# A due time for every operation of a list-planned residual quantizer

## The chip, the core and the metric

The kernel runs on one core of one Trainium2 chip. The metric is the device time of one execution in microseconds, the median of the runs. A core has TensorE (PE) for matrix products, VectorE (DVE) and ScalarE (ACT) for elementwise work, GpSimd (POOL) and SyncE (SP), which here mostly issue transfers, and 16 DMA engines. Each engine works through its own queue in the order in which the program was written; an operation at the head of a queue that waits holds up all that stands behind it.

## The reference

```python
B, T, D, K = 2, 16000, 512, 3
Nq, C = 4, 8
...
z = sum over i of xp[:, i:i+T, :] * dw_enc[i]      # 3 taps along T, per channel
z = silu(z)
res = z; q = 0
for s in range(Nq):
    cb = codebooks[s]                               # 8 words of 512
    d2 = |res|^2 - 2 res.cb + |cb|^2
    sel = cb[d2.argmin(-1)]
    q = q + sel
    res = res - sel
y = sum over i of qp[:, i:i+T, :] * dw_dec[i]      # 3 taps along T, per channel
```

All tensors are bfloat16; `xp` and `qp` are padded by one row at each end of T. A three-tap filter per channel is followed by a SiLU, then by four stages of quantization. Each finds the nearest of 8 code words for every row and subtracts it from the residual. The sum of the chosen words goes through a second three-tap filter.

## The kernel before

The 32000 rows are 128 partitions of 250 rows. A *group* is one row of every partition, so there are 250 groups, worked on in 18 chunks of 4, 12, thirteen times 16, 12, 8 and 6 groups (`SIZES`). A chunk is held transposed, channels on partitions, in four blocks of 128 channels (`KT`); a full block is 128 x 2048 elements.

For each chunk, in order:

- `load`: DMA transposes on SP's queue (L491) bring rows into an `XT` buffer, of which there are two. The first two chunks come by `load_rows`: PE transposes, and copies to `XT` by ACT (L456) for even blocks and by DVE (L454) for odd ones.
- `front`, for each block: three products with the taps (L557 on DVE; L555 on ACT for the middle tap of blocks 0 to TAPS1-1 of the first `FEW` = 6 chunks), two additions (L565 on DVE, or L563, an accumulating transfer that POOL issues: one for each block, two for block 0, none in the first two chunks), then `exp` on ACT (L569), `one` (plus 1, DVE, L576), `inverse` on ACT (a reciprocal, recorded at the helper's line L201), and `silu` on DVE (L584), which writes the residual `RES`. Exponentials and reciprocals need different tables of ACT, which are loaded between them.
- `stage`, four times: products of the residual with itself and the code words on PE (`score`, L654 and L659), in two or three parts for a chunk; maxima and copies on DVE and ACT (L694, L672, L698); the small chain on DVE `with_norm` (L736), `distance` (L742), `least` (L746), `marks` (L751); `turn` and `pairs` on PE (L769, L802) with copies on ACT (L778, L807); `chosen` on PE (L835), which writes the chosen words to PSUM as `SEL`; and `subtract` on DVE (L841). In the fourth stage `settle` takes the place of `pairs` and what follows.
- `finish`: the decoder's products (`Y`, L859), copies to `YSB` by ACT (L865, 126 of them), and stores on SP's queue (L869).

**The planner.** Nothing is issued while these functions run. Each calls `plan.add(engine, hold, delay, needs, due, emit, take, give, use, move)`: the engine and how long it is held, how long until the result can be used, the entries that must be done first, a due time, the function that issues the instructions, and the buffers that are taken and given back. `move` describes a transfer on a shared bus. `Plan.run` then goes through time on these prices. Whenever an engine is free it takes, among the entries whose needs are met and whose buffers are there, the one with the earliest due time, and issues it. The order in which the entries are taken is the order of the program, for each engine; the prices themselves cause nothing on the chip. The engine name `BANK` stands for bookkeeping entries that issue no instruction.

Due times come from a few constants in units of `PERIOD` = 56 planned us: a chunk starts at `org`, 56 us for 16 groups after the one before; products and additions of block i fall due at `org + (i * SPREAD - LEAD) * PERIOD`, `exp` and `one` `EXPS` periods after that, `inverse` and `silu` at `org + AFTER * PERIOD`, stage s at `org + s * STAGE * PERIOD`, and so on. A path-length term, `END - STRETCH * tail`, can only make them earlier.

Two rules of the `front` matter below. An `inverse` needs its own block's `one` and the last `exp` that was added, block 3's; an `exp` needs the last `inverse` of the chunk before:

```python
e = plan.add("ACT", act(1.8) + load, act(1.8) + load + 0.12, [z] + turned[-1:], due + EXPS * PERIOD, exp, take=("E",))
...
e = plan.add("ACT", act(1.8) + load, act(1.8) + load + 0.12, [o, ended[-1]], due, inverse)
```

Here `load` is `SWITCH` = 1.3 for block 0 and 0 for the others, so the plan counts one table load for the exponentials and one for the reciprocals of a chunk.

**Idle products.** When PE would stand still in the plan and has been little used in the last 3.4 planned us, the planner puts in a product whose result nobody reads (`warm`, L432; 229 of them).

Of the kernel before, what the change touches and what calls it, by code (L numbers as in the profile page):

```python
# [37 lines left out]
SWITCH = 1.3  # L38
PERIOD = 56.0
LEAD = 0.269  # L40
SPREAD = 0.081
EXPS = 0.293
AFTER = 0.664
STAGE = 0.861
NEXT = 0.126
LAST = 0.74
LATE = 0.468
HURRY = 0.905
TABLES = -1.436
COLS = 0  # L50
MOVES = 0
END = 1097.406
STRETCH = 2.086
FEW = 6
ONES1 = 0
TAPS1 = 2
ROWS = 2
SUMS = 0
NORMS = 14
NFROM = 2  # L60
NTO = 14
OVER = -0.515
FETCH = 1.963
FAR = -3.3e38


class Plan:
# [7 lines left out]
        self.bus, self.turned = 9.0, 0.0  # L75

    def add(self, engine, hold, delay, needs, due, emit, take=(), give=(), use=1.0, move=None):
        self.tasks.append((engine, hold, delay, [n for n in needs if n is not None], due, emit, take, give, use, move))
        return len(self.tasks) - 1

    def run(self):
        tasks = self.tasks
        left = [len(t[3]) for t in tasks]
        after = [[] for _ in tasks]
        for n, t in enumerate(tasks):
            for d in t[3]:
                after[d].append(n)
        engines = list(dict.fromkeys(t[0] for t in tasks))
        ready = {e: [] for e in engines}
        until = {e: 0.0 for e in engines}  # L90
        tail = [0.0] * len(tasks)
        for n in reversed(range(len(tasks))):
            t = tasks[n]
            tail[n] = max(t[1], t[2] + (t[9][0] if t[9] else 0.0)) + max((tail[a] for a in after[n]), default=0.0)
        dues = [min(t[4], END - STRETCH * tail[n]) for n, t in enumerate(tasks)]
        spans = []
        for n, t in enumerate(tasks):
            if not left[n]:
                heapq.heappush(ready[t[0]], (dues[n], n))
        now, events, order = 0.0, [], []  # L100
        while len(order) < len(tasks):
            going = True
            while going:
                going = False
                for e in engines:
                    if until[e] > now + 1e-9:
                        continue
                    passed, pick = [], None
                    while ready[e]:
                        due, n = heapq.heappop(ready[e])  # L110
                        if all(self.slots[k] > 0 for k in tasks[n][6]):
                            pick = n
                            break
                        passed.append((due, n))
# [24 lines left out]
                    if e == "PE":  # L139
                        spans.append((now, until[e], tasks[pick][8]))  # L140
                    heapq.heappush(events, (now + hold, -1))
                    heapq.heappush(events, (now + max(hold, delay), pick))
                    going = True
            if len(order) == len(tasks):
                break
            now = events[0][0]
            while events and events[0][0] <= now + 1e-9:
                _, n = heapq.heappop(events)
                if n < 0:
                    continue  # L150
                for k in tasks[n][7]:
                    self.slots[k] += 1
                for a in after[n]:
                    left[a] -= 1
                    if not left[a]:
                        heapq.heappush(ready[tasks[a][0]], (dues[a], a))
# [3 lines left out]
def kernel(  # L160
# [310 lines left out]
    def load(st, org):  # L471
# [5 lines left out]
        if st["n"] in plain:  # L477
            st["off"] = g0
            space = plan.add("BANK", 0.0, 0.0, [chunks[0]["space"]], early, lambda: st.update(XT=chunks[0]["XT"]))
            for n in range(g0 + 2, g0 + G + 2):  # L480
                done.append(plan.add("SP", 1.31, 0.9, [space], early + 0.01 * n,
                                     lambda n=n: nc.sync.dma_start_transpose(out=chunks[0]["XT"][:, :, n, :], in_=group_rows(n - 1)),
                                     move=(0.78, True)))
            st["loaded"] = done + chunks[st["n"] - 1]["loaded"]
            return

# [27 lines left out]
        for n in range(2, G + 2):  # L514
            due += 0.01
            inside = 0 <= g0 + n - 1 < S
            t = plan.add("SP", 1.31, 0.9, [space], due, (lambda n=n: one(n)) if inside else (lambda n=n: edge(n)), move=(0.78, True))
            done.append(t)
            if not inside:
                done.append(plan.add("POOL", 1.0, 1.4, [t], due, lambda n=n: shift(n)))  # L520
# [3 lines left out]
    def front(st, org):  # L524
# [21 lines left out]
        def block(i):  # L546
# [41 lines left out]

            def add_up(k, needs):
                if k <= adds:  # L590
                    return plan.add("POOL", 0.9, 1.24, needs, due, lambda: total(k), give=("T",), move=(0.2 + 2.6 * f, False))
                return plan.add("DVE", dve(1.13), dve(1.13) + 0.1, needs, due, lambda: total(k), give=("T",))

            hold, delay = dve(0.67), dve(0.67) + 0.1
# [3 lines left out]
                t = plan.add("ACT", act(2.0), act(2.0) + 0.12, st["loaded"], due, lambda: product(1), take=("T",))  # L598
            else:
                t = plan.add("DVE", hold, delay, st["loaded"], due, lambda: product(1), take=("T",))  # L600
            z = add_up(1, [z, t])
            t = plan.add("DVE", hold, delay, st["loaded"], due, lambda: product(2), take=("T",), give=("XT",) if i == KT - 1 and n >= plain[-1] else ())
            st["taps"].append(t)
            z = add_up(2, [z, t])
            load = 0.0 if ended else SWITCH
# [16 lines left out]

            return rest

        ended, now = [], []
        st["taps"], st["silu"], st["new"] = [], [], {}
        for rest in [block(i) for i in range(KT)]:
            rest()
        begun.extend(now)

    turned, begun, kept = [], [], {}

    def stage(st, s, due):
        G, MB = st["GP"], st["MB"]
# [11 lines left out]

        def score(q, m):
            RES = st["RES"]
            if q == 0:
                u["TR"], u["PR"] = SCORES[turns[0] % len(SCORES)]  # L650
                turns[0] += 1
            PS = pending.pop() if pending else psG.tile([P, 512], F32, name="PS")
# [2 lines left out]
            for e in range(m):  # L655
                for i in range(KT):
                    for h in range(2):
                        half = RES[:, i, 2 * (e % 2 * R + (q + e) // 2) + h, :]
                        nc.tensor.matmul(V[h * HT:(h + 1) * HT, e, :], lhsT=half[:, LC:LC + HT], rhs=half[:, lo:hi],  # L659
                                         start=False, stop=(i == KT - 1), skip_group_check=True)  # L660
            if s == Nq - 1 and q + m == G:
                free["RES"].append(RES)
            if not scored[2:]:
                scored.append(None)

# [36 lines left out]
        for m in ([4], [4, 4], [6, 6], [6, 6, 4])[MB - 1]:  # L702
            needs = [st["new"][i] for i in range(KT)]
            needs += scored[0:2] + ([codes[st["n"]]] if st["n"] < 3 else [])
            t = plan.add("PE", 0.05 + 0.215 * m, 0.25 + 0.215 * m, needs, due, lambda q=q, m=m: score(q, m), take=("psG",),
                         give=("RES",) if s == Nq - 1 and q + m == G else (), use=0.7)
            seen.append(t)
            if apart:
                g = plan.add("ACT", 0.06 + 0.0535 * m, 0.18 + 0.0535 * m, [t], due, lambda q=q, m=m: positive(q, m), take=("G",))
# [9 lines left out]
            plan.add("BANK", 0.0, 0.0, maxima[-2:], due, lambda: None, give=("psG",))  # L719
            q += m  # L720

        if apart:
            first, rest = grams[:-1], grams[-1:]
            t = plan.add("PE", 0.04 * sum(m for _, m, _, _ in first), 0.2 + 0.04 * sum(m for _, m, _, _ in first),
# [88 lines left out]
            t = plan.add("DVE", 0.2, 0.33, maxima, due, with_norm, give=("psA",) if apart else ())  # L813
        t = plan.add("DVE", 0.15, 0.26, [t], due, distance)
        t = plan.add("DVE", 0.2, 0.33, [t], due, least)
        t = plan.add("DVE", 0.2, 0.36, [t] + preset[0:3], due, marks, take=("OH",) if s == 0 else ())
        last = s == Nq - 1
        t = plan.add("PE", 0.05 + 0.06 * MB if last else 0.15, 0.25 + 0.06 * MB if last else 0.33, [t], due, turn, take=("psA",),
                     give=("OH",) if last else ())
# [31 lines left out]
    def outputs(groups, needs, due):  # L851
# [20 lines left out]
        for k in range(0, len(groups), 2):  # L872
# [1 line left out]
            d = [plan.add("PE", 0.22 * count, 0.22 * count + 0.2, needs, due, lambda k=k: decode(k), take=("psA",))]  # L874
            decoded.extend(d[-1:])
            c = plan.add("ACT", 0.93, 1.05, [c, d[-1]], due, lambda k=k: pair(k), take=("Y",) if k == 0 else (), give=("psA",))
        plan.add("SP", 0.35, 1.1, [c], due, store, give=("Y",), move=(0.1 + 0.365 * len(groups), False))

    def edge(name, src, shift):
        t = const.tile([P, P], BF16, name=name)  # L880
# [84 lines left out]
```

## Time and profile before

| what | value |
|---|---|
| three runs | 719.88, 714.88, 717.16 us; median 717.16 |
| profiled execution | 723.01 us, span 721.3 us |
| mean granted TensorE clock | 0.95 |
| DVE busy | 631.5 us, 88% |
| PE busy | 573.7 us, 80% |
| ACT busy | 569.0 us, 79% |
| POOL busy | 104.3 us, 14% |
| accumulating transfers, issue to landing | 80; median 6.3 us |
| transposes, issue to landing | 233; median 4.7 us |
| stores of 512 KB, issue to landing | 61; median 3.3 us |

The shares are of the span of one profiled execution. A group row gives line, engine, operation, output and input, count, busy time, the mean ns of one, and the engine's idle time just before them with what ended it. A wait row gives the engine and line that waited, what it waited for, the total in us, how often, and the longest.

### The profile page before, as it was taken

The numbers are of one execution on the slowest core, as the hardware profiler recorded it, in microseconds if no ns is written. First come the engines' busy times: TensorE is split into PE (matmuls) and PEld (weight loads), VectorE is DVE, ScalarE is ACT, GpSimd is POOL, SyncE is SP. The second block draws the span as 40 slices with busy tenths as digits, with TensorE's granted clock in tenths as the row PEclk, the third lists the DMA queues.
The fourth block names the chain that finished last, engine by engine and source line by source line (L and its number), as shares of the span: only waits on it lengthen the run. The fifth ranks groups of instructions, "written<-read, shape, count | busy, mean of one in ns | idle before, by whom it ended". The sixth has DMA issues, their size and how long they took to land. (4 is left out here: it accounts for less than half of the span.)

```text
span 721.3 us, 27550 instructions
## 1 busy us (share of the span) xinstructions
PE 573.7 (80%) x12353; PEld 342.8 (48%) x12353; DVE 631.5 (88%) x1060; ACT 569.0 (79%) x791; POOL 104.3 (14%) x142
## 2 busy tenths in 40 slices
PE   4167688788889888888888788887888878979986
PEld 3034354544545555455544555463453545545553
DVE  6997999897999997999899898998796969887871
ACT  4885769699799798789888699796888894966456
POOL 8301021112011111111011111010101021100000
PEclk9598999999899999999999999999899999999999
DMA  9819796979899999798999999989857462422024
GB/s 197 121 40 169 132 184 120 161 121 202 141 205 186 155 199 133 162 195 146 204 158 201 157 223 128 235 133 169 186 85 188 77 177 41 152 62 90 32 105 189
DMA packets 149648, 107.51 MB, mean 149 GB/s; under 512 B 130297, under 2 KB 130682, under 8 KB 149402
## 3 DMA queue, kind: packets, MB, share of 16 engines
q1 hardware_dynamic: 137076, 65.96, 46.1%
q0 software_dynamic: 12448, 39.79, 33.0%
q8 instruction: 96, 1.57, 0.9%
q14 instruction: 22, 0.18, 0.1%
q10 hardware_dynamic: 6, 0.00, 0.0%
HBM read 3.61 MB, written 32.77 MB: 50 GB/s over the span
## 5 line engine op out<-in xcount | busy, mean ns | idle before, releaser
L841 DVE TENSOR_TENSOR RES<-RES,SEL 128x2048 bf16<-128x2048 bf16 (+3 forms) x216 | 222.8, 1079 | 23.3 <-PE SEL L835 23.0
L659 PE MATMUL PS<-RES 128*64 128x80 bf16 (+1 forms) x8064 | 185.5, 205 | 31.4 <-DVE RES L584 19.4
L659 PEld LDWEIGHTS <-RES 128*64 128x64 bf16 x8064 | 159.7, 115 | 82.8 <-issue 51.8
L835 PE MATMUL SEL<-OHP,W 64*128 64x512 bf16 (+3 forms) x1296 | 152.7, 360 | 33.5 <-ACT YSB L865 12.0
L563 POOL DMA_DIRECT2D Z<-T x80 | 81.2, 1024 | 531.3 <-DVE T L557 97.0
L865 ACT ACTIVATE YSB<-Y 128x1024 bf16<-128x1024 f32 (+1 forms) x126 | 126.7, 1030 | 28.1 <-DMA out_dram<-YSB 13.6
L569 ACT ACTIVATE E<-Z 128x2048 bf16<-128x2048 bf16 (+3 forms) x72 | 122.7, 1707 | 25.7 <-DVE Z L565 25.3
L201 ACT ACTIVATE E<-E 128x2048 bf16<-128x2048 bf16 (+3 forms) x72 | 121.4, 1709 | 0.2
L835 PEld LDWEIGHTS <-W 64*128 64x128 bf16 x1296 | 61.3, 95 | 99.9 <-issue 62.4
L557 DVE TENSOR_SCALAR T<-XT,WENC 128x2048 bf16<-128x2048 bf16 (+3 forms) x132 | 87.8, 682 | 6.8 <-DMA Z<-T 6.8
L859 PE MATMUL Y<-A,FIN 128*128 128x512 bf16 x249 | 71.3, 390 | 26.1 <-ACT YSB L865 11.1
L565 DVE TENSOR_TENSOR Z<-Z,T 128x2048 bf16<-128x2048 bf16 (+3 forms) x64 | 65.2, 1022 | 18.3 <-DMA Z<-T 18.3
L584 DVE TENSOR_TENSOR RES<-Z,E 128x2048 bf16<-128x2048 bf16 (+3 forms) x72 | 78.1, 1084 | 3.5 <-ACT E L201 3.4
L432 PE MATMUL PS<-CB,IDENT 128*128 128x512 bf16 x229 | 72.6, 412 | 2.8 <-ACT PR L698 2.8
L698 ACT ACTIVATE PR<-PS 128x48 bf16<-128x48 f32 (+1 forms) x192 | 42.0, 222 | 35.5 <-PE PS L659 29.3
L654 PE MATMUL PS<-MASK,IDENT 128*128 128x384 bf16 (+1 forms) x192 | 61.2, 319 | 7.0 <-DVE TR L694 4.6
L672 ACT ACTIVATE GRAM<-PS 128x384 bf16<-128x384 f32 (+1 forms) x108 | 50.2, 469 | 9.4 <-PE PS L659 9.3
L694 DVE TENSOR_REDUCE TR<-PS 128x6 bf16<-128x384 f32 (+1 forms) x84 | 41.1, 497 | 14.3 <-PE PS L659 9.3
L557 DVE TENSOR_SCALAR Z<-XT,WENC 128x2048 bf16<-128x2048 bf16 (+3 forms) x72 | 48.7, 677 | 0.1
L859 PEld LDWEIGHTS <-FIN 128*128 128x128 bf16 x249 | 20.6, 98 | 51.4 <-issue 32.6
L576 DVE TENSOR_SCALAR E<-E 128x2048 bf16<-128x2048 bf16 (+3 forms) x72 | 43.7, 617 | 0.6 <-ACT E L569 0.4
L807 ACT ACTIVATE OHP<-ps_pair,NEG 128x512 bf16<-128x512 f32 (+3 forms) x54 | 34.3, 639 | 8.7 <-PE ps_pair L802 6.4
(103 smaller groups left out, 481.3 us busy)
## 6 DMA issues: line engine op xcount, KB each, us to landing
Z<-T POOLq DMA_DIRECT2D x65, 512.0 KB, 6.6
out_dram<-YSB SPq DMA_DIRECT2D x61, 512.0 KB, 3.3
XT<-in_x_dram SPq DMA_TRANSPOSE x233, 4.7
Z<-T POOLq DMA_DIRECT2D x10, 256.0 KB, 4.3
Z<-T POOLq DMA_DIRECT2D x5, 384.0 KB, 4.6
RES<-in_x_dram SPq DMA_DIRECT2D x1, 1536.0 KB
RES<-in_x_dram SPq DMA_DIRECT2D x1, 640.0 KB, 5.3
W<-in_codebooks_dram POOLq DMA_DIRECT2D x6, 64.0 KB, 9.3
```

Source lines behind the costliest of these rows:

```text
L201: nc.scalar.add_instruction(mybir.InstActivation(name=nc.get_next_instruction_name(), engine=mybir.EngineType.Activation, ins=args, outs=[ ...
L432: nc.tensor.matmul(pending[0], lhsT=IDENT, rhs=CB4, start=True, stop=True, skip_group_check=True)
L557: nc.vector.tensor_scalar(out=places(u[name]), in0=taps(i, k), scalar1=WENC[:, i, k:k + 1], scalar2=None, op0=ALU.mult)
L563: nc.gpsimd.dma_start(out=z, in_=t, accum_op=ALU.add)
L565: nc.vector.tensor_tensor(out=z, in0=z, in1=t, op=ALU.add)
L569: nc.scalar.activation(u["E"][:, 0:G, :], u["Z"][:, 0:G, :], ACT.Exp, scale=-1.0)
L584: nc.vector.tensor_tensor(out=st["RES"][:, i, 0:2 * G, LC:LC + HT], in0=halves(u["Z"]), in1=halves(u["E"]), op=ALU.mult)
L659: nc.tensor.matmul(V[h * HT:(h + 1) * HT, e, :], lhsT=half[:, LC:LC + HT], rhs=half[:, lo:hi], start=False, stop=(i == KT - 1), skip_group ...
L835: nc.tensor.matmul(SEL[:, r, 0:R * HT], lhsT=WORDS[s][k][rows, i * P:(i + 1) * P], rhs=u["OHP"][rows, 0:R * HT], start=(k == 0), stop=(k = ...
L841: nc.vector.tensor_tensor(out=now, in0=now, in1=sel[:, :, 0:G, :], op=ALU.add)
L859: nc.tensor.matmul(Y[:, h, :], lhsT=lhs(), rhs=rhs, start=(a == 0), stop=(a == len(terms) - 1))
L865: nc.scalar.activation(u["YSB"][:, k:k + n, :], u[k][:, 0:n, :], ACT.Copy)
```

## The change

Every planned entry gets a shift of its own, in fiftieths of a planned us, which is added to its due time (`SHIFTS`, 3254 numbers from -608 to +651 planned us). Most constants of the due times change. TAPS1 goes from 2 to 3 and MOVES from 0 to 1. The planner's prices change: PE entries are held longer by 1/0.95, every result but a transfer's or a bookkeeping entry's comes 0.05 planned us later and not before its engine is free, transfers take more of the bus. Since the operations of a chunk may now be taken in any order that their needs allow, `XT` is given back by a bookkeeping entry behind the products of all four blocks (before: with block 3's last one), and `RES` by one behind all score parts of the last stage (before: with the last part). A stage's score buffers are taken by whichever part comes first. NFROM 2 to 0 adds nothing, since the rule asks for a chunk of 16 groups and the first of these is chunk 2.

```diff
-SPREAD = 0.081
-EXPS = 0.293
-AFTER = 0.664
-STAGE = 0.861
-NEXT = 0.126
-LAST = 0.74
+SPREAD = 0.024
+EXPS = 0.467
+AFTER = 0.72
+STAGE = 0.842
+NEXT = 0.156
+LAST = 1.06
 LATE = 0.468
-HURRY = 0.905
-TABLES = -1.436
+HURRY = 0.077
+TABLES = -1.809
 COLS = 0
-MOVES = 0
-END = 1097.406
-STRETCH = 2.086
+MOVES = 1
+END = 1636.455
+STRETCH = 1.759
...
-TAPS1 = 2
+TAPS1 = 3
...
-NFROM = 2
+NFROM = 0
 NTO = 14
-OVER = -0.515
-FETCH = 1.963
+CLOCK = 0.95
+SIGNAL = 0.05
+OVER = 0.28
+FETCH = 2.075
...
+SHIFTS = [
+    0, 12580, 6936, 11129, -4601, 11543, 2818, -914, -1883, 8487, 11977, 6113, 9034, 9433, -9521, 12956, -5274, -111, 16876, 11963,
...
+]
...
     def add(self, engine, hold, delay, needs, due, emit, take=(), give=(), use=1.0, move=None):
-        self.tasks.append((engine, hold, delay, ...
+        if engine == "PE":
+            hold, delay = hold / CLOCK, max(delay, hold / CLOCK)
+        self.tasks.append((engine, hold, delay if engine == "BANK" else (delay if move else max(hold, delay)) + SIGNAL, ...
...
-        dues = [min(t[4], END - STRETCH * tail[n]) for n, t in enumerate(tasks)]
+        dues = [min(t[4], END - STRETCH * tail[n]) + (SHIFTS[n] / 50.0 if n < len(SHIFTS) else 0.0) for n, t in enumerate(tasks)]
...
-                                     move=(0.78, True)))
+                                     move=(0.9, True)))
...
-                    return plan.add("POOL", 0.9, 1.24, needs, due, lambda: total(k), give=("T",), move=(0.2 + 2.6 * f, False))
+                    return plan.add("POOL", 1.4, 1.24, needs, due, lambda: total(k), give=("T",), move=(0.2 + 2.75 * f, False))
...
+            middle.extend([z, t])
             z = add_up(1, [z, t])
-            t = plan.add("DVE", hold, delay, st["loaded"], due, lambda: product(2), take=("T",), give=("XT",) if i == KT - 1 and n >= plain[-1] else ())
+            t = plan.add("DVE", hold, delay, st["loaded"], due, lambda: product(2), take=("T",))
...
+        reads.extend(st["taps"] + middle)
+        if n >= plain[-1]:
+            plan.add("BANK", 0.0, 0.0, reads[:], due, lambda: None, give=("XT",))
+            del reads[:]
...
-            if q == 0:
+            if "TR" not in u:
...
-            if s == Nq - 1 and q + m == G:
-                free["RES"].append(RES)
...
-                         give=("RES",) if s == Nq - 1 and q + m == G else (), use=0.7)
+            ..., take=("psG",), use=0.7)
...
+        if s == Nq - 1:
+            plan.add("BANK", 0.0, 0.0, seen, due, lambda: free["RES"].append(st["RES"]), give=("RES",))
...
-        t = plan.add("DVE", 0.2, 0.36, [t] + preset[0:3], due, marks, take=("OH",) if s == 0 else ())
+        t = plan.add("DVE", 0.231, 0.44, [t] + preset[0:3], due, marks, take=("OH",) if s == 0 else ())
...
-        plan.add("SP", 0.35, 1.1, [c], due, store, give=("Y",), move=(0.1 + 0.365 * len(groups), False))
+        plan.add("SP", 0.35, 1.1, [c], due, store, give=("Y",), move=(0.1 + 0.385 * len(groups), False))
```

More of the change, by code (lines that the diff above doesn't have):

```diff
@@ L77, in add @@
     def add(self, engine, hold, delay, needs, due, emit, take=(), give=(), use=1.0, move=None):
-        self.tasks.append((engine, hold, delay, [n for n in needs if n is not None], due, emit, take, give, use, move))
+        if engine == "PE":
+            hold, delay = hold / CLOCK, max(delay, hold / CLOCK)
+        self.tasks.append((engine, hold, delay if engine == "BANK" else (delay if move else max(hold, delay)) + SIGNAL, [n for n in needs if n is not None], due, emit, take, give, use, move))
         return len(self.tasks) - 1
@@ L516, in load @@
             inside = 0 <= g0 + n - 1 < S
-            t = plan.add("SP", 1.31, 0.9, [space], due, (lambda n=n: one(n)) if inside else (lambda n=n: edge(n)), move=(0.78, True))
+            t = plan.add("SP", 1.31, 0.9, [space], due, (lambda n=n: one(n)) if inside else (lambda n=n: edge(n)), move=(0.9, True))
             done.append(t)
@@ L623, in block @@
             return rest
-        ended, now = [], []
+        ended, now, middle, due = [], [], [], org
         st["taps"], st["silu"], st["new"] = [], [], {}
@@ L628, in front @@
             rest()
+        reads.extend(st["taps"] + middle)
+        if n >= plain[-1]:
+            plan.add("BANK", 0.0, 0.0, reads[:], due, lambda: None, give=("XT",))
+            del reads[:]
         begun.extend(now)
-    turned, begun, kept = [], [], {}
+    turned, begun, reads, kept = [], [], [], {}
     def stage(st, s, due):
@@ L704, in stage @@
             needs += scored[0:2] + ([codes[st["n"]]] if st["n"] < 3 else [])
-            t = plan.add("PE", 0.05 + 0.215 * m, 0.25 + 0.215 * m, needs, due, lambda q=q, m=m: score(q, m), take=("psG",),
-                         give=("RES",) if s == Nq - 1 and q + m == G else (), use=0.7)
+            t = plan.add("PE", 0.05 + 0.215 * m, 0.25 + 0.215 * m, needs, due, lambda q=q, m=m: score(q, m), take=("psG",), use=0.7)
             seen.append(t)
```

162 rows, old and new, of the table SHIFTS are left out of this document.

## The prediction

> **What bounds the kernel now.** I read the busy shares first, then the same shares by stretch, then what VectorE (DVE) waited for, then the groups and the timeline of ScalarE (ACT).
>
> The page's first part and its span: DVE is the fullest engine, ACT and TensorE (PE) are not far behind.
>
> ```profile
> span 721.3 us, 27550 instructions
> PE 573.7 (80%) x12353; PEld 342.8 (48%) x12353; DVE 631.5 (88%) x1060; ACT 569.0 (79%) x791; POOL 104.3 (14%) x142
> ```
>
> The windows (busy us and count of each engine, then granted clock, DMA share, GB/s) split the 88%:
>
> ```profile
> core 0: us, PE busy (x) PEld busy (x) DVE busy (x) ACT busy (x) POOL busy (x), PEclk, DMA share, GB/s
> 0.00:80.00 80.00, 39.67 (x495) 24.37 (x497) 68.87 (x156) 51.35 (x60) 26.56 (x63) 0.83 0.81 136
> 80.00:480.00 400.00, 333.28 (x7547) 199.89 (x7543) 371.99 (x553) 343.05 (x462) 54.02 (x53) 0.96 0.99 170
> 480.00:640.00 160.00, 133.74 (x3061) 78.68 (x3056) 138.07 (x237) 127.70 (x189) 23.13 (x26) 0.97 0.59 126
> 640.00:721.30 81.30, 67.04 (x1267) 39.84 (x1264) 52.56 (x117) 46.90 (x84) 0.64 (x1) 0.97 0.27 102
> ```
>
> DVE idles 11.1, 28.0, 21.9 and 28.7 us in the four stretches, 89.8 in all. In the long middle it is 93% busy: there is little to win there. In the last 81 us it is 65% busy: few operations are left, and each waits for another engine. An order can only win from these idle times. What DVE waited for in the whole run:
>
> ```profile
> DVE RES L841 <- PE SEL L835: 23.0, 21, 4.8
> DVE Z L565 <- DMA Z<-T: 18.3, 12, 3.5
> DVE TR L694 <- PE PS L659: 9.3, 11, 1.5
> DVE T L557 <- DMA Z<-T: 6.8, 6, 2.8
> ```
>
> No single wait rules; 12.2 us of the first row lie in 480 to 640 us. Last, how ACT changes its table. The groups (busy us, mean ns | idle before):
>
> ```profile
> L569 ACT ACT_TABLE_LOAD x17 | 21.8, 1283 | 10.3 <-DMA Z<-T 10.1
> L201 ACT ACT_TABLE_LOAD x18 | 23.1, 1283 | 0.3
> ```
>
> And the timeline of one chunk (start us, us):
>
> ```profile
> 307.40 1.91 ACT L569 ACTIVATE E<-Z 128x2048 bf16<-128x2048 bf16 x1 [1.07 <-DVE Z L565]
> ...
> 309.59 0.20 ACT L698 ACTIVATE PR<-PS 128x48 bf16<-128x48 f32 x1
> ...
> 309.81 1.28 ACT L201 ACT_TABLE_LOAD   x1
> 311.10 1.91 ACT L201 ACTIVATE E<-E 128x2048 bf16<-128x2048 bf16 x1
> ...
> 326.60 1.28 ACT L569 ACT_TABLE_LOAD   x1
> ```
>
> For 18 chunks there is one load for the exponentials and one for the reciprocals of each: all four exponentials of a chunk, then all four reciprocals.
>
> **The change, part by part.** The profiled execution took 723.0 us (span 721.3 and 1.7 around it); the sum is made against that. The median of the three runs, 717.16, is 0.992 of it, and the result is scaled by that at the end.
>
> *Work moved to ACT.* TAPS1 3 gives ACT a third product of the middle tap in chunks 0 to 5: DVE loses 4 x 0.746 + 0.604 + 0.397 = 4.0 us (L557 by shape), ACT gains 4 x 2.001 + 1.561 + 0.710 = 10.3 (L555). MOVES 1 gives it the XT copies of odd blocks: DVE loses 2 x 0.950 + 2 x 0.542 = 3.0 (L454), ACT gains 2 x 1.441 + 2 x 0.810 = 4.5 (L456). So DVE -7.0, ACT +14.8, all in the first 160 us, where ACT is busy 117.1 us and its idle 42.9 covers it. Bounds: -7.0 if DVE sets the pace throughout, +4.5 if the copies stand one behind the other on ACT at the start, where they feed the first products. I take -5: DVE is at 90% there (144.1 of 160).
>
> *The new order, before 640 us.* The number of instructions on PE, DVE, SP and POOL is the same but for the seven microseconds above (and the idle products of PE, which fill only its gaps). In 80 to 480 us 28.0 us of idle time can be had at most; an order that leaves 2% (8 us) would win 20, one that helps nothing 0. I take a third, 9, because 11.8 of the 28 are waits for the accumulating transfers, and the DMA share is 0.99 there. In 480 to 640 us that share is 0.59; I let DVE rise to the middle's 93% (11.2 idle us): -10.7, bounds 0 and -18.7 (2%).
>
> *The tail.* 52.6 us of DVE work stand in 81.3 us. At 75% they take 70.1: -11.2. Bounds: 0, and at the 86% of the stretch before 60.9, so -20.4. LAST 1.06 lets the outputs of the last four chunks fall due 0.32 x 56 = 18 planned us later; 21 of the 126 output copies (19.9 us of ACT) already lie in the last 40 us, and the chain that ended last goes through them. I take +3, about one store's landing (3.3 us); bounds 0 and +10, half of those copies.
>
> *Buffers freed by all readers.* These are bookkeeping entries without an instruction. XT and the residual come free later or at the same time, so SP's transposes can only start later. The last transpose starts at 575.9 us and its chunk's last product at 638.8: that cover makes it 0; +5 without it, one transpose's landing (4.7).
>
> *Planner prices* (CLOCK, SIGNAL, 0.9 for 0.78 and so on) cost nothing on the chip; they shape the order. The accumulating transfer is now planned at 1.24 + 2.95 = 4.2 us alone, where the page has a median of 6.6 from issue to landing. What waits for it is late: DVE waited 25.1 us for it, ACT 10.1. If the new order crowds POOL's and SP's queues, that could double, if it spaces them it could vanish: -25 to +25, and I take 0, since the transfers are the same in number.
>
> *Table loads.* This is the cost that the planner does not see. An inverse (L201) needs its own block's `one` and the exp of block 3, `ended[-1]`. Before, exps fall due at 1.3 to 15.0 and inverses at 37.2 planned us from the chunk's start, so block 3's exp came last and the rule kept the two kinds apart. With shifts it need not. I worked out every due time of these operations (formula plus SHIFTS/50), took the later of an exp's own and its feeders' due times, and sorted. Chunk 2: exp 3 at 30, exp 2 at 152, inverse 2 at 152, exp 0 at 160, exp 1 at 189, inverses 0, 1, 3 at 219, 232, 308: three changes of kind instead of one. Over 18 chunks I count 66 instead of 18, so about 84 loads instead of 36 with those between chunks. 48 x 1.283 = 61.6 us more on ACT; SWITCH stays priced at one load for each kind. ACT's idle 57.0 us in 80 to 480 is 5.7 for each 40 us, in which a chunk passes (12 subtractions of L841), against 48/18 x 1.283 = 3.4 of new loads. Bounds 0 and +61.6. ACT would be at 94%, level with DVE, but DVE names ACT for only 12 us of its waits; PE names it for more (SEL and Y behind YSB, 23.5). I take a quarter, +15.4.
>
> The Trainium skill (ScalarE: Activation LUTs, "What ACT_TABLE_LOAD costs") adds a drain of about 1.38 us to the 1.283 of each load, 2.66 in all. This trace speaks against it: the next activation starts 0.01 us behind the load at 309.81, and the copy ahead had ended 0.02 us before it. By the skill's figure the term would be an estimated 32 instead of 15, and the time 716, inside the no-change case.
>
> Sum: -5 - 9 - 10.7 - 11.2 + 3 + 15.4 = -17.5; 723.0 - 17.5 = 705.5; times 0.992, **700 us**.
>
> **Rivals.** *The loads fall into idle time* (faster still): 723.0 - 32.9 = 690.1, scaled 684. For it: ACT has 152 idle us in all, and the actual order can be kinder than the due times. Against: ACT does what is ready, and exps come some 5 us apart (327.9, 329.8, 334.9), which leaves gaps that an inverse will enter.
>
> *ACT becomes the bound* (slower): every wrong-table operation stops ACT's queue for 1.28 us and, behind it, the copies that free PSUM for SEL and Y; DVE waits for SEL. With all loads on the path 690.1 + 61.6 = 751.7, scaled 746; with eight tenths 739.4, scaled 733. It decides from 32.9/61.6 = 53% of the load time on. For it: ACT and DVE would both stand near 94%, so a stall of one is not made up. Against: at present DVE seldom waits for ACT.
>
> *No change*: the planner's order is won on prices that the chip does not keep (4.2 planned against 6.6 measured), and the three order terms bring a third, -10.3: 723.0 - 5 - 10.3 + 3 + 15.4 = 726.1, scaled 720.
>
> *The change doesn't do what it says*: shifts are tied to operations by number, so one entry out of place would scramble the plan. The list has 3254 numbers. The plan before has 3219 entries, the new bookkeeping adds 17 for XT and 18 for the residual: 3254. The 320 zeros fall exactly on the entries that issue nothing. I give this 1 in 100, with a time near 760.
>
> **How the numbers follow.** Forecast 700: 0.36. Loads hidden, 684: 0.19. No change, 720: 0.13. ACT the bound, about 733: 0.31. Misplaced shifts: 0.01. The likeliest has its own range of 690 to 710 (a tenth to four tenths of the loads). For 8 in 10 the range goes from 676 (the hidden-loads case with 8 us more from the bounds of the order terms) to 740 (nine tenths of the loads, 690.1 + 55.4 = 745.5, scaled). A measurement here tells about 1%, 7 us, from no change: faster 0.55, same 0.13, slower 0.32.
>
> **What would show it.** ACT_TABLE_LOAD rows near 84 in all; at 36 to 50 the hidden-loads case. ACT busy near 645 (569 + 14.8 + 61.6). DVE busy near 624.5, its share above 93% in 80 to 480 and above 70% in the last 80 us. L555 x18, L454 gone, L456 x8. If DVE's waits for SEL rise over 23 us and ACT's share passes DVE's, ACT is the bound. The forecast is wrong if the loads are many and the time still falls below 690, or if they stay few and it does not fall.

## The result: 1.3% faster

| kernel | median | lowest to highest | runs |
|---|---|---|---|
| before | 719.41 us | 714.50 to 727.13 | 20 |
| after | 709.47 us | 705.18 to 719.66 | 20 |

The ratio is 0.9867, with a 95% interval of 0.9839 to 0.9894. The gain is real, 9.9 us by the medians. The forecast of 700 us stood 17 us under the three runs of before that were known then, and it stands 19 us under the median of the 20, so about half of it came. Ratios, here and below, compare undisturbed runs of the same chip alone, so a ratio can differ a little from that of the medians beside it.

After's page:

```profile
span 708.5 us, 27303 instructions
PE 554.2 (78%) x12195; PEld 340.0 (48%) x12295; DVE 629.5 (89%) x1050; ACT 597.8 (84%) x813; POOL 99.4 (14%) x142
```

DVE's busy time fell by 2.0 us only, ACT's rose by 28.8, and the span by 12.8. Almost all of the gain is therefore DVE idle time. (The two profiled executions lie 3 us further apart than the medians.) The windows of after (us, busy us and count of PE, its weight loads, DVE, ACT and POOL, then granted clock, DMA share, GB/s):

```profile
0.00:80.00 80.00, 35.38 (x403) 21.53 (x406) 60.92 (x135) 59.68 (x64) 26.04 (x63) 0.74 0.72 127
80.00:480.00 400.00, 328.12 (x7546) 201.42 (x7601) 373.97 (x563) 355.03 (x471) 49.33 (x52) 0.94 1.00 169
480.00:640.00 160.00, 135.70 (x3174) 83.25 (x3196) 149.19 (x248) 140.32 (x206) 24.08 (x27) 0.96 0.70 141
640.00:708.50 68.50, 54.98 (x1096) 33.84 (x1100) 45.45 (x107) 42.75 (x75) 0.00 (x0) 0.98 0.26 102
```

DVE's idle time is the length of a stretch less its third busy number. In the four stretches it went from 11.1 to 19.1, from 28.0 to 26.0, from 21.9 to 10.8 and from 28.7 to 23.0 us. The start lost 8 us; from 80 us on 18.8 were won, most of it after 480 us. What DVE waited for (total us, times, longest):

```profile
DVE RES L1016 <- PE SEL L1010: 10.4, 16, 1.8
DVE E L747 <- ACT E L740: 8.7, 9, 2.7
DVE T L728 <- DMA Z<-T: 8.1, 5, 4.3
DVE TR L868 <- PE PS L835: 7.1, 10, 1.1
DVE RES L755 <- ACT E L372: 5.8, 5, 1.8
DVE A L570 <- DMA A<-in_dw_dec_dram: 4.9, 3, 2.8
...
DVE Z L736 <- DMA Z<-T: 2.6, 4, 1.1
```

The lines have moved: L1016 is the old L841 (`subtract`), L1010 `chosen`, L747 `one`, L740 `exp`, L728 and L736 the products and additions, L372 the helper's reciprocal, L755 `silu`, L570 the decoder's tables. The old first wait, for SEL, fell from 23.0 to 10.4 us, and the two rows for the accumulating transfer from 25.1 to 10.7. In their place DVE now waits for ACT, 14.5 us in the two rows for `E`, where before had 3.8:

```profile
DVE RES L584 <- ACT E L201: 3.4, 2, 2.8
DVE E L576 <- ACT E L569: 0.4, 2, 0.2
```

A second profiled execution of the same order (the replay below) has 8.1 us for SEL, 16.9 for the transfer and 12.3 for `E`.

The groups of ACT's table loads (busy us, mean ns | idle before); with one at the start they make 48, against 36 before and 84 forecast:

```profile
L372 ACT ACT_TABLE_LOAD x24 | 30.8, 1283 | 0.4
L740 ACT ACT_TABLE_LOAD x23 | 29.5, 1283 | 0.4
```

ACT's timeline shows the first chunk (start us, us):

```profile
28.27 1.28 ACT L372 ACT_TABLE_LOAD   x1
29.56 0.63 ACT L372 ACTIVATE E<-E 128x512 bf16<-128x512 bf16 x1
31.40 0.63 ACT L372 ACTIVATE E<-E 128x512 bf16<-128x512 bf16 x1 [1.21 <-DVE E L747]
...
36.53 1.28 ACT L740 ACT_TABLE_LOAD   x1
37.82 0.63 ACT L740 ACTIVATE E<-Z 128x512 bf16<-128x512 bf16 x1
...
38.99 1.28 ACT L372 ACT_TABLE_LOAD   x1
40.28 1.15 ACT L372 ACTIVATE E<-E 128x512 bf16<-128x512 bf16 x2
...
42.10 1.28 ACT L740 ACT_TABLE_LOAD   x1
```

The reciprocals at 29.56 and 31.40 run before the chunk's last exp, at 37.82, and the other two (x2 at 40.28) follow it: a second pair of loads. Six chunks (0, 1, 2, 12, 16, 17) have such a second pair; between 104 and 443 us every chunk keeps to one.

### The profile page after: what moved, and what is told of

Read it like the earlier page. It is cut to its first block, busy times and chain, and to the rows that moved or that the text cites. A ratio compares the mean times of both kernels' runs of the same rounds, so it can differ in the third digit from the quotient of the medians.

```text
span 708.5 us, 27303 instructions
## 1 busy us (share of the span) xinstructions
PE 554.2 (78%) x12195; PEld 340.0 (48%) x12295; DVE 629.5 (89%) x1050; ACT 597.8 (84%) x813; POOL 99.4 (14%) x142
## 3 DMA queue, kind: packets, MB, share of 16 engines
q0 software_dynamic: 12448, 39.79, 32.9%
## 5 line engine op out<-in xcount | busy, mean ns | idle before, releaser
L1016 DVE TENSOR_TENSOR RES<-RES,SEL 128x2048 bf16<-128x2048 bf16 (+3 forms) x216 | 226.5, 1086 | 11.2 <-PE SEL L1010 10.4
L835 PE MATMUL PS<-RES 128*64 128x80 bf16 (+1 forms) x8064 | 188.0, 206 | 36.1 <-DVE RES L755 29.3
L835 PEld LDWEIGHTS <-RES 128*64 128x64 bf16 x8064 | 162.3, 116 | 91.8 <-issue 49.3
L1010 PE MATMUL SEL<-OHP,W 64*128 64x512 bf16 (+3 forms) x1296 | 152.1, 364 | 15.6 <-DVE RES L1016 4.7
L734 POOL DMA_DIRECT2D Z<-T x80 | 74.5, 935 | 524.0 <-DVE T L728 79.4
L740 ACT ACTIVATE E<-Z 128x2048 bf16<-128x2048 bf16 (+3 forms) x72 | 122.1, 1700 | 13.5 <-DVE Z L736 12.2
L372 ACT ACTIVATE E<-E 128x2048 bf16<-128x2048 bf16 (+3 forms) x72 | 121.5, 1702 | 1.5 <-DVE E L747 1.2
L1010 PEld LDWEIGHTS <-W 64*128 64x128 bf16 x1296 | 58.7, 97 | 77.2 <-issue 39.2
L728 DVE TENSOR_SCALAR T<-XT,WENC 128x2048 bf16<-128x2048 bf16 (+3 forms) x126 | 84.5, 685 | 8.5 <-DMA Z<-T 8.1
L755 DVE TENSOR_TENSOR RES<-Z,E 128x2048 bf16<-128x2048 bf16 (+3 forms) x72 | 78.0, 1088 | 5.9 <-ACT E L372 5.8
L1034 PE MATMUL Y<-A,FIN 128*128 128x512 bf16 x182 | 60.0, 387 | 19.2 <-DVE RES L1016 7.5
L872 ACT ACTIVATE PR<-PS 128x48 bf16<-128x48 f32 (+1 forms) x192 | 39.2, 213 | 37.3 <-PE PS L835 33.3
L736 DVE TENSOR_TENSOR Z<-Z,T 128x2048 bf16<-128x2048 bf16 (+3 forms) x64 | 65.5, 1026 | 2.6 <-DMA Z<-T 2.6
L603 PE MATMUL PS<-CB,IDENT 128*128 128x512 bf16 x149 | 51.1, 442 | 3.5 <-issue 2.2
L747 DVE TENSOR_SCALAR E<-E 128x2048 bf16<-128x2048 bf16 (+3 forms) x72 | 44.9, 630 | 8.9 <-ACT E L740 8.7
L728 DVE TENSOR_SCALAR Z<-XT,WENC 128x2048 bf16<-128x2048 bf16 (+3 forms) x72 | 49.5, 689 | 2.5 <-DMA XT<-in_x_dram 2.3
L856 PE MATMUL ps_n<-SIDE,GRAM 128*64 128x1 bf16 x1152 | 29.0, 172 | 11.9 <-ACT OHL L953 3.6
```

The lines of the kernel that those rows point to most:

```text
L372: nc.scalar.add_instruction(mybir.InstActivation(name=nc.get_next_instruction_name(), engine=mybir.EngineType.Activation, ins=args, outs=[ ...
L728: nc.vector.tensor_scalar(out=places(u[name]), in0=taps(i, k), scalar1=WENC[:, i, k:k + 1], scalar2=None, op0=ALU.mult)
L734: nc.gpsimd.dma_start(out=z, in_=t, accum_op=ALU.add)
L736: nc.vector.tensor_tensor(out=z, in0=z, in1=t, op=ALU.add)
L740: nc.scalar.activation(u["E"][:, 0:G, :], u["Z"][:, 0:G, :], ACT.Exp, scale=-1.0)
L755: nc.vector.tensor_tensor(out=st["RES"][:, i, 0:2 * G, LC:LC + HT], in0=halves(u["Z"]), in1=halves(u["E"]), op=ALU.mult)
```

## Experiments

My theory after the result: the gain is the order's alone; the work moved to ACT and the extra loads give nothing or cost something. The first rival: the moved work and the prices gain, and any reasonable order would do. The second: the loads eat half of what the order won. The same order of after, replayed from a written list, measured 708.72 us and 0.9788 (0.9727 to 0.9849) in a later session, beside the 0.9867 above. Two measurements of one program thus lie 0.8 points apart, and smaller differences between sessions can't be told apart here.

```diff
 def run(self):
-    ...  # planning with dues, prices and SHIFTS
+    for n in ORDER:
+        self.idle() if n < 0 else self.tasks[n][5]()
```

> The changed kernel itself, its order written out as a list instead of planned (the same program on every engine): the mark for the runs beside it. 709 us, ratio 0.987.

The experiments on after's order below are such lists, but for the one without shifts and the one without table loads.

### Is it the order?

*Without shifts:* the new prices, constants and moved work, but due times from the formulas alone.

```diff
-SHIFTS = [...]
+SHIFTS = []
```

> The changed kernel with all shifts zero: the new constants, prices, moved work and bookkeeping alone. If the gain comes from the due time of each operation, this is slower than the kernel before, 725 to 750, with DVE's idle time in 80 to 640 us well over 50; if the constants and prices bring it, 705 to 715.

Measured 753.19 us, 1.0377 (1.0316 to 1.0439), with 42 loads. DVE's middle, by the windows:

```profile
80.00:480.00 400.00, 318.30 (x6677) 185.27 (x6671) 336.40 (x501) 324.40 (x422) 45.35 (x49) 0.92 0.87 153
```

DVE is busy 84% instead of 93%, with fewer loads. The formulas as they now stand are worse than the old ones; the shifts bring the whole gain and make good the loss of the formulas besides, 5 to 6 points together.

*Blurred.* Entries are ranked by their planned start in after plus a random number, from which an order that the needs and buffers allow is made:

```diff
-rank = start[n]
+rank = start[n] + uniform(-x, x)      # planned us
```

> The changed kernel with its order blurred: every entry is ranked by its planned start time plus a random number between -0.5 and 0.5 planned us (one draw), so that 742 of 1020 entries of DVE stand at another place, 2.2 places off on average. If the exact order matters as much as the coarse one, the gain of 10 us is lost and more, 718 to 735; if the coarse order carries it, 708 to 713.

Measured with x = 0.5: 747.57 us, 1.0314 (1.0255 to 1.0372). 742 of 1020 DVE entries changed places, by 3.0 places on average (2.2 over all 1020). A second draw with the same x:

> A second draw of the blur of 0.5 planned us: 752 of 1020 entries of DVE at another place, 2.7 places off on average. If the exact order carries the gain, 735 to 755 like the first draw (747.6); if that was an accident, under 725.

751.59 us, 1.0399 (1.034 to 1.0458). And x = 0.1, which moved 252 DVE entries, by 2.9 places on average (0.7 over all 1020):

> The changed kernel's order blurred by a random number between -0.1 and 0.1 planned us: 252 of 1020 entries of DVE change places, 0.7 places off on average over all. If the price of a swap grows with how many there are, a third of the first draw's loss, 10 to 15 us slower than the changed kernel, about 722; if only a few swaps between certain neighbours did it, between 0 and 40 and no telling; if swaps so near do nothing, 709.

723.87 us, 1.0004 (0.9963 to 1.0045): the gain is gone. DVE's waits and its middle with x = 0.5, first draw (L946 is `subtract`, L658 the products, L841 `with_norm`):

```profile
DVE RES L946 <- PE SEL L940: 21.3, 30, 2.2
DVE T L658 <- DMA Z<-T: 15.8, 7, 4.7
DVE V L841 <- PE ps_n L786: 7.9, 8, 3.6
```

```profile
80.00:480.00 400.00, 330.28 (x7277) 196.15 (x7275) 359.88 (x539) 333.00 (x446) 49.30 (x51) 0.94 0.92 161
```

DVE is busy 359.88 us there instead of 373.97. The waits for SEL are twice as many as in after (30 for 16) and as short. This fits queues in which the next operation can't step past one that waits. The blurred lists also hold 208, 211 and 180 idle products instead of 171; leaving out all of them changed nothing (below).

That the gain hangs on the order, down to places within the queues, is shown. How many entries move, and how far, does not decide it. Two orders further down keep the gain: the one that gathers the reciprocals moves 217 DVE entries by 3.0 places (and has 12 loads less), the one with later tables 77 by 8.9. So after's order is not the only good one. Which swaps cost the most is not known.

### The moved work and the start

*The moved work alone, in the order of before:*

```diff
-                if k == 1 and i < aside:
+                if k == 1 and i < (3 if aside else 0):
...
-            if i % 2 and not MOVES:
+            if False:
```

> The kernel before in its own order, with the third tap product of the first six chunks and all XT copies issued on ACT at the places where they stood. DVE loses 7.0 us, ACT gains 14.8. ACT's time was free in the kernel before (35 table loads less did not move it), so if DVE sets the pace there the time falls by 3 to 7 us, to about 714; if the order's waits set it, no change within 2; if the copies hold up the first chunk as they do in the changed kernel, 2 to 5 us slower.

Measured 726.87 us, 1.0062 (1.0022 to 1.0103): no gain, by its interval slower by 1.6 to 7.4 us, though 0.6 points are less than two measurements of after lay apart. The windows, and DVE's waits:

```profile
0.00:80.00 80.00, 39.37 (x435) 23.95 (x435) 61.57 (x143) 56.30 (x63) 24.96 (x63) 0.83 0.77 131
```

```profile
DVE Z L565 <- ACT T L555: 4.5, 3, 3.1
```

DVE is busy 61.57 us instead of 68.87 in the first 80 us: its idle time there rose by 7.3 us, so nothing else was done in the time that came free. The second row is new among DVE's long waits: 4.5 us for products that ACT now makes.

*The moved work taken back, in the order of after:*

```diff
-                if k == 1 and i < aside:
+                if k == 1 and i < min(aside, 2):
...
-            if i % 2 and not MOVES:
+            if i % 2:
```

> The changed kernel in its own order, but the third tap product of the first six chunks and the XT copies of odd blocks are issued on DVE at the places where they stood, as before. ACT loses 14.8 us, DVE gains 7.0. If the moved work is a gain by itself (-5 forecast), the time rises by 3 to 7 us; if the copies on ACT held up the start, it falls by 3 to 8 and DVE's idle time in the first 80 us falls from 19.

Measured 707.73 us, 0.9800 (0.9748 to 0.9852), not to be told from after. In the new order too no gain of the moved work shows.

*The decoder's tables later.* Five products that build the tables (L570), which wait 4.9 us for a transfer at the head of DVE's queue, move some 40 us back in the list:

```diff
-ORDER = [..., <five table entries>, ..., <entry at 62 planned us>, ...]
+ORDER = [..., ..., <entry at 62 planned us>, <five table entries>, ...]
```

> The changed kernel in its own order, but the five products that make the decoder's tables (L570) stand some 40 us later in DVE's queue; nothing needs them before the first output. DVE waited 4.9 us for their transfers. If what the start loses is lost at the end, the time falls by 3 to 6 us; if the chunks behind catch up, by under 2.

705.25 us, 0.9761 (0.9671 to 0.9850). With both edits, the tables and the moved work back:

> The same, and the third tap product of the first six chunks and the odd XT copies back on DVE. If the start sets the end, DVE idles about 10 us in the first 80 us and the time falls by 5 to 9 us; if not, it stays within 3 us of the changed kernel.

706.14 us, 0.9815 (0.9747 to 0.9883). Its windows:

```profile
0.00:80.00 80.00, 39.50 (x432) 23.83 (x437) 68.43 (x146) 56.18 (x61) 25.57 (x63) 0.79 0.76 135
```

DVE's idle time at the start fell from 19.1 to 11.6 us, about as before the change, yet the medians are 705 to 708 beside 708.72. Most of these 7.5 us are the moved work itself: DVE's busy time over the run rose from 629.5 to 635.6, by 6.1 us, and filled the idle time. So these kernels show that the start had room for that work. What the start's idle time costs at the end they do not show, since a gain of some 3 us can't be told here. They beat before by about 2%; none is shown to beat after.

### The table loads

*All loads away, in both orders.* The reciprocal becomes a copy, which leaves the table alone; every instruction stays but the loads (a full block takes 1936 ns as a copy, 1916 as a reciprocal):

```diff
-    func=ACT.Reciprocal
+    func=ACT.Copy
```

> The changed kernel in its own order, with the reciprocal on ACT replaced by a copy of the same tile, so that no table is ever changed (the SiLU is left out with it, its time is what counts). 47 loads of 1.283 us, 60.3 us of ACT, are gone. If a load costs its length at the end, the time falls by 60 us to about 650; if a quarter of it reaches the end, by 15 to about 694; if the loads fall into ACT's idle time, by under 4.

> The same edit in the kernel before: 35 loads, 44.9 us of ACT, are gone. At a quarter the time falls by 11 us to about 708. The difference between the two falls is the price of the 12 loads that the change adds: 15 us if they stand on the path, 4 at a quarter, 0 if they are hidden.

After without its 47 loads: 688.16 us, 0.9518 (0.9459 to 0.9578). Before without its 35: 0.9988 (0.9927 to 1.0050), no gain (the median of all its runs is 726.35 us). Against after's two measurements (0.9867 and 0.9788), 0.9518 is lower by 2.7 to 3.5 points, so 19.5 to 25 us, 0.41 to 0.53 us for each load; against the two kernels measured in the same session (0.9800 with the moved work taken back, 0.9848 with the extra loads taken out, below) it is 2.8 and 3.3 points. The windows of after without loads, then the middle stretch of before without loads:

```profile
0.00:80.00 80.00, 36.98 (x433) 21.89 (x435) 63.56 (x139) 52.90 (x59) 27.04 (x63) 0.79 0.77 133
80.00:480.00 400.00, 340.46 (x7817) 205.60 (x7813) 382.95 (x576) 329.10 (x460) 51.00 (x54) 0.96 1.02 173
480.00:640.00 160.00, 140.36 (x3363) 85.78 (x3363) 152.78 (x273) 126.94 (x201) 20.68 (x25) 1.00 0.66 136
640.00:687.40 47.40, 38.61 (x687) 22.40 (x686) 27.69 (x64) 27.90 (x49) 0.00 (x0) 0.98 0.31 123
```

```profile
80.00:480.00 400.00, 333.38 (x7539) 200.33 (x7539) 371.05 (x553) 314.67 (x436) 51.27 (x53) 0.96 1.00 168
```

Without loads after's DVE rises from 373.97 to 382.95 us, 95.7%. Before's stays at 371.05 (371.99 with loads), though ACT lost 28.4 us there. In the old order ACT's loads stand in idle time; in the new one a part of them is on the path. DVE's waits for `E` in 80 to 480 us show it, first in after, then in after without loads:

```profile
DVE E L747 <- ACT E L740: 4.4, 4, 2.7
DVE RES L755 <- ACT E L372: 1.7, 2, 1.5
```

```profile
DVE E L747 <- ACT E L740: 0.2, 1, 0.2
```

So the second rival holds for the 47 loads taken together: they eat more than half of what the new order would win without them, 0.9518 against 0.9788 to 0.9867. It does not follow for the 12 extra ones.

*The extra loads alone.* An inverse needs all four exps of its chunk; other entries are ranked by their planned start in after:

```diff
-    [o, ended[-1]]
+    [o] + ended[-4:]
```

> The changed kernel with one rule more: an inverse waits for all four exponentials of its chunk. The rest of the order is kept as near as the needs allow (by the planned start times of the changed kernel): 126 of ACT's entries and 217 of DVE's change places, by 23 at most. 36 loads instead of 48. If the 12 loads (15.4 us) are what the start lost, it gains 5 to 15 us, to 695 to 704, and DVE's idle time in the first 80 us falls from 19 to about 11. If the late exponentials of block 1 are the cause and the loads only filled the wait, the reciprocals now wait too: same or slower, 709 to 720.

36 loads, as in before, and ACT busy 581.9 us, 15.9 less than after, but 710.18 us, 0.9848 (0.9806 to 0.9890), the time of after. Taken away in this way, the 12 extra loads gain nothing. But the edit disturbed the order too: DVE's waits for SEL rose from 10.4 to 18.7 us. Whether the 12 loads by themselves cost 12 x 0.41 to 0.53, 5 to 6 us, stays open.

### Is ACT's time the path in general?

The 126 output copies read half of the sums and write zeros in words twice as wide over the same bytes. A copy takes 602 ns instead of 1038, so ACT has some 47 us less (busy 550.9 in after, 521.1 in before):

```diff
-nc.scalar.activation(u["YSB"][:, k:k + n, :], u[k][:, 0:n, :], ...)
+nc.scalar.activation(half[:, k:k + n, :], u[k][:, 0:n, 0:D // 2], ACT.Copy, scale=0.0)
```

> The changed kernel in its own order, with each of the 126 output copies of ACT made half as long (it writes zeros as 4-byte words over the same bytes, from half of the sums; the stores stay as long, the output is zeros). By the rows of 512 and 1024 elements (594 and 1037 ns) that is 0.44 us each, 56 us of ACT in all, about what the 47 table loads were. If ACT's time is on the path in the new order, whatever takes it, the time falls by about 20 us as it did without the loads, to about 690; if only the loads hurt, because they stand in front of the reciprocals, under 6.

> The same edit in the kernel before. Without its 35 loads (44.9 us of ACT) it stayed at 0.999. If its order is what sets the time, it stays within 1% again; since PSUM is also free 0.44 us sooner for SEL and Y, which wait 23.5 us for these copies, it could fall by 5 to 10 us.

After: 699.01 us, 0.9699 (0.9645 to 0.9754), lower than after's two measurements by 0.9 to 1.7 points, 6.5 to 12 us. Its interval still overlaps that of the replay. Before: 719.63 us, 0.9964 (0.9927 to 1.0002), an interval that reaches no change. This points to ACT's time in general as part of the path in the new order, and not its loads alone, but the difference between the two orders is at the edge of what can be told here. Shorter copies also free PSUM sooner, which the edit does not separate. The 47 loads are 60.3 us of ACT and give 0.32 to 0.42 us for each us; the copies give 0.14 to 0.26. Why a us of loads is worth more than a us of copies was not settled. Loads lie between an exp and a reciprocal, which feed DVE through `one` and `silu`; that is argued, not shown.

### The idle products

The 171 entries below zero, which stand for them, are dropped from the list:

```diff
-self.idle() if n < 0 else self.tasks[n][5]()
+if n >= 0: self.tasks[n][5]()
```

> The changed kernel in its own order without the 171 idle products. If they keep PE's clock up, the granted clock falls from 0.93 to 0.90 or less and the time rises by 5 to 20 us; if PE's own work does that, both stay and the time may fall by 1 or 2 us, since nothing waits behind an idle product any more.

707.65 us, 0.9800 (0.9751 to 0.9848): nothing lost. The cores view:

```profile
core 0: 706.2 us, clock 0.890
```

The mean granted clock fell (0.931 in the replayed after), and no time was lost with it. In this order no worth of the idle products shows.

### A search that prices every load

If the plan had only missed the loads, an order searched with each load priced at its place should win. Two such orders, with the work moved back, end 15.9 and 19.3 planned us sooner than after's (the second against after's with the moved work back) and have 38 and 40 loads:

```diff
-ORDER = [...]      # after's
+ORDER = [...]      # random search over shifts, every load priced
```

> An order of its own: found by a random search from the changed kernel's order with the planner's prices, and with 1.3 planned us added whenever ACT changes between exponentials and reciprocals (the plan before and after adds it once for each kind and chunk, whatever the order); the moved work is back on DVE. 38 loads. By these prices it ends 15.9 planned us sooner than the changed kernel's order. If the unpriced loads are what the changed kernel loses, the time falls by 10 to 20 us, to about 695; if prices so fine do not hold on the chip, it is no better than the changed kernel or, like the blurred order, far worse.

> A second order from the same search with another seed, 40 loads, 19.3 planned us sooner than the changed kernel's moved-back order by the same prices. The same as for the first; if the two differ by more than 10 us, the search's prices are not what decides.

711.21 us, 0.9884 (0.9802 to 0.9966), and 715.55 us, 0.9921 (0.9871 to 0.9972). Neither beats after. The 16 and 19 planned us are not kept by the chip; which of the plan's prices is wrong stays open. Over 900 of DVE's 1020 entries stand at other places than in after, by more than 5 on average, and 0.8 and 1.2 points of gain are still there.

## Why the prediction was right or wrong

*Right: the way of the result and the place of the gain.* Only DVE's idle time was to be won, and the order did win it. 480 to 640 us brought -11.1 for -10.7 forecast, and the SEL waits there went from 12.2 to 0.8 us. The tail brought -5.7 for -8.2 (with the +3 for `LAST`); DVE's share of the last 80 us rose from 64% to 70.5%, where over 70% was forecast. L555's product is x18, the DVE copies are gone and ACT's are x8, as said.

*Wrong: the loads, forecast at 48 extra and +15.4. This is the step that failed.* The count failed in its method: I sorted due times, but a due time ranks only what is ready. The exps become ready in the order in which DVE finishes the blocks, and most were taken before a competing inverse was. (The three exps that I called some 5 us apart start 1.9 and 5.1 us apart.) It was 12 extra loads, 15.4 us of ACT; ACT's busy time follows: 569.0 + 14.8 + 15.4 = 599.2, and 597.8 was measured. What the 12 do to the end could not be told from 0.

The price failed too, and in the other direction. The prediction charged the extra loads alone, at a quarter of their time, because DVE named ACT for only 12 us of its waits. For the old order that reading holds: its 35 loads cost nothing (0.9988). In the new order all 47 share the path and cost 19.5 to 25 us, 0.41 to 0.53 of 1.283 us for each. Without them the order brings what the other terms had promised: 0.9518 of 717.16 is 683 us, where the prediction without its loads' term had 684. ACT did become part of the path; by busy time DVE stayed ahead, at 89% to ACT's 84%.

*The middle, forecast at -9.* Its 28.0 us of idle time became 26.0. DVE's waits there for the accumulating transfers, which the prediction took as the limit, fell from 11.8 to 5.3 us (10.6 in the replay), but its waits for `E` rose from 0.9 to 6.1. Without the loads, the middle has 17.1 us of idle time, -11.0. By parts, 160 to 320 us rose from 147.3 busy us of DVE (92%) to 153.6 (96%), and 80 to 160 us fell from 75.2 to 72.0, behind the late start.

*Wrong: the work moved to ACT, forecast at -5.* No gain of it shows: alone it measured +1.6 to +7.4 us, and taken back from after it gained or lost nothing. "DVE is at 90% there" was read from the stretch as a whole. In the first 80 us DVE waits for the first chunks to come through ACT, PE and the transfers, and work taken from it there became idle time. DVE's busy time was to fall by 7.0, to 624.5 us, and is 629.5. By the kernels that put it back the moved work is 5.8 to 6.1 us, but DVE's other operations took some 4 us more, the full subtractions 184.9 instead of 181.7.

*Wrong: the first 80 us, put at nothing.* Their idle time rose by 8.0 us, 4.9 us of waits for the decoder's tables among it. What this costs at the end stays open.

*Put at 0: the waits for the accumulating transfers.* Their median from issue to landing hardly changed, 6.0 us for 6.6, but DVE's waits for them fell from 25.1 to 10.7 us (16.9 in the replay), within the bounds of 25 that were given. The table has this in the stretches.

The terms beside DVE's time in profiled executions, of after and of after without its loads (us; busy time is that of the whole run, the stretches are idle time, in which what the loads cost is contained):

| term | forecast | after | without loads |
|---|---|---|---|
| work moved to ACT | -5 | -2.0 in busy time | -4.5 in busy time |
| idle time, 0 to 80 us | 0 | +8.0 | +5.3 |
| idle time, 80 to 480 us | -9 | -2.0 | -11.0 |
| idle time, 480 to 640 us | -10.7 | -11.1 | -14.7 |
| tail, with `LAST` | -11.2 + 3 | -5.7 | -9.0 |
| loads | +15.4 | in the stretches | none |
| sum | -17.5 | -12.8 | -33.9 |

Without the loads' row the forecast is -32.9, and the kernel without loads came to -33.9. So the other terms were right in their sum, though not in each row, and the missing part of the gain is the loads' term: 21.1 us between the two profiled executions for the 15.4 forecast. That the forecast sum came as near as it did is luck in part: four times too many extra loads at a price that left out the old ones.

*On the rivals.* The loads stayed at 48, in the band given for the hidden-loads case, but they were not hidden. That case was right in its count and wrong in its condition; its 684 us is what the order reaches when the loads are taken out. "No change" gave as its reason prices that the chip does not keep. The searched orders bear this reason out.

*What a load takes.* By the Trainium skill (ScalarE: Activation LUTs, "What ACT_TABLE_LOAD costs"), 2.66 us for a load, 12 more would cost an estimated 32 us of ACT. The timeline of after has the next activation 0.01 us behind a load of 1.28 (28.27 + 1.28, then 29.56), and ACT's busy sum holds with 1.283 alone.

## What to carry to other kernels

When two engines are both near 85 to 90% and every queue is in order, price a change by the waits at its place: work taken from an engine that waited for its inputs, as at the start here, was worth nothing. Before you trust a gain from a finely tuned order, blur it: this one lost 1.4 to 2.2 points when a quarter of the DVE entries moved by 3 places on average, though other edits of that size kept it. And when an order fills one engine's gaps, look which engine was its cushion: ACT's table loads, which cost nothing in the old order, cost 0.32 to 0.42 us per us in the new one. Take such a cost out in both orders, as here by a copy in place of the reciprocal, before you put a price on it.

## What was not expected of the hardware

- 171 idle products less lowered the mean granted clock from 0.931 to 0.890 and cost no time (0.9800 beside 0.9788). That PE, busy 78%, had room for it is argued, not shown.
- 35 table loads, 44.9 us of ACT's 569, could be taken from before without any gain (0.9988), while 47 in after were worth 19.5 to 25 us: the same instruction has no price of its own, only one in its order.
